# Attention feeding an MLP: the weight-mixing steps are pinned to their place and moved later, attention starts batch 1 at half rate

## The chip, the cores and the metric

The kernel runs on one NeuronCore of one Trainium2 chip. The metric is device time of one execution, in microseconds (us). The core has five engines with one instruction queue each: TensorE (PE; its weight loads are listed apart as PEld), VectorE (DVE), ScalarE (ACT), GpSimd (POOL) and SyncE (SP). In this kernel SP issues nearly all DMAs. An engine takes its queue in order, so an instruction that waits holds up everything behind it.

## The reference

```python
def _attn_ref(q, k, v):                       # 8 batches, 12 heads, 448 tokens, head size 64
    S = q.shape[2]
    scale = 1.0 / np.sqrt(q.shape[-1])
    scores = scale * np.matmul(q, k.transpose(0, 1, 3, 2)) - np.log(S)
    attn = 1.0 / (1.0 + np.exp(-scores))
    return np.matmul(attn, v)

def _moe_ref(x, w_in, w_out):                 # 3584 tokens, 768 -> 2048 -> 768
    h = x @ w_in
    g = np.where(h >= 1, h, np.where(h <= -1, 0.0, (h + 1) ** 2 / 4.0))
    return g @ w_out
```

The attention output of the 12 heads of a batch, laid side by side, is `x` of the MLP. All of it is float32 in and out.

## The kernel before, in words

**Stages.** The batches go one after another. While PE does the MLP of batch b, attention of batch b+1 is woven in, in "pieces": a batch has 6 pairs of heads of 5 pieces, 30 in all (`NPIECE`). A piece is a score product (L393 to L411), a sigmoid (ACT L440 or L443), for later pairs a split of the result into two f16 halves (ACT L451, DVE L452), and the product with v (L484). The MLP of a batch is a list of units. Batch 0 has 48 "up" units (h = x w_in, L708) and 24 "down" units for the first eight of sixteen chunks of w_out (L744; the sums are put aside in DRAM, `part`). Batch 1 has 24 up units, 24 down units that end batch 0 with the other eight chunks, 24 up units and 48 down units, 120 in all. From batch 2 on the up product is done in seven block products instead of eight (L674), which needs mixed sums of w_in.

**Splitting.** Products of f32 accuracy are made of f16 halves. `split` turns a chunk f of a weight into its high half (ACT L270 or L266) and its low half (DVE L271, or POOL L267 and L268 for chunks 1, 7 and 13). The f32 copy of a chunk lies where the halves of the next chunk go, so chunk f+1's ACT step follows chunk f's DVE step: the splits are one long ladder. The first eight chunks of w_out are split under scale `wo0`, the others under `wo1`.

**Mixing.** `mix(i)`, i from 0 to 7, builds the block sums of w_in's chunks i and i+8. DVE adds the halves of both chunks (L618, twice, into tile `mixa`), forms four sums (L622 to L625), ACT and DVE split the result (L631, L632, into `mixs`), SP sends it to DRAM (L635, `blocks`), DVE scales the unmixed parts (four of L641, into `mixp`), and SP sends these (L644). The three tiles share a ring of two buffers (`raww`): the next mix's `mixa` takes the buffer of this one's `mixs` and so waits until its DMA has landed, and its `mixs` takes the buffer of `mixp`. The first three sets of `blocks` are loaded back over w_in at the end of batch 1 (`load_set`, L650), and the scaled x blocks of batch 2 (ACT L533, DVE L534) go over w_in's chunks 10 to 16, so all mixes must have read w_in by then. In the program mix(i) stands at unit `MIX0 + i * (MIX1 - MIX0) // 8` of batch 1: units 8, 17, 27, 36, 46, 56, 65, 75.

**What sets the order.** A planner orders each engine's queue ahead of the run: it goes through the program with priorities in program order and a model of times, and gives an engine with nothing ready an instruction from further down. So an instruction can be placed ahead of its place in the program when its inputs and its buffer are ready. `tc.keep_in_program_order(...)` takes that freedom from an instruction: it stays behind the instructions that precede it in the program on its engine, as done for the weight loads. The order is then fixed for the run, whatever the real times are.

**Pacing of attention.** For each batch `share` gives the part of the batch's attention pieces that are to be done by unit u; it is the running sum of per-unit rates, all 8 in the kernel before, so the 30 pieces are spread evenly over the first `last` units (102 in batch 1).

**Names.** PSUM tiles: `psc` scores (2 buffers), `pav` attention output (1), `mo` with `ph`, `po` and `pm` (3 buffers in one ring). `bend` is the nonlinearity: ACT L721 and L724, DVE L722, L723, L725. `start_blocks` (L516, then `diag` L164) and `finish_blocks` find the scale of x for batch 2: PE L174, DVE L175, `x_s` L134, then L533 and L534.

Of the kernel before, what the change touches and what calls it, by code (L numbers as in the profile page):

```python
# [34 lines left out]
NA = 8  # L35
# [18 lines left out]
SB = 2  # L54
QA = 17
QT = 3
WOP = 6
MIXP = 0
CORN = 10
TP = 1  # L60

DW = 8
MIX0 = 8
MIX1 = 85
Q_PRIO = 72

PM = 9
# [5 lines left out]
def sigmoid_attention_mlp(ctx: ExitStack, tc: tile.TileContext, first_qvk, qkv, w_in, w_out, out_t):  # L73
    nc = tc.nc
# [438 lines left out]
    def start_blocks():  # L513

        xm1 = sml_p.tile([P, 1], F32, tag="xm1", name="xm1", bufs=1)
        nc.vector.tensor_reduce(out=xm1, in_=state["xm"], axis=AX.X, op=ALU.max)  # L516
        return xm1, on_diagonal(xm1)
# [79 lines left out]
    def mix_scales():  # L597

        def keep(tag, in0, s1, op0, s2=None, op1=None):
            n = len(mixed)  # L600
            mixed[tag] = t = mixes[:, n : n + 1]
            nc.vector.tensor_scalar(out=t, in0=in0, scalar1=s1, scalar2=s2, op0=op0, **({"op1": op1} if op1 else {}))
            return t

        low = keep("low", wi.scale[0], wi.scale[1], ALU.min, 0.25, ALU.mult)
        keep("inv", wi.inv[0], wi.inv[1], ALU.max, 4.0, ALU.mult)
        to = [keep("to%d" % k, low, wi.inv[k], ALU.mult) for k in range(2)]
        keep("ratio", wi.scale[1], wi.inv[0], ALU.mult)
        keep("minus", mixed["ratio"], -1.0, ALU.mult)
        mixed["to"] = to  # L610

    def mix(i):

        to, ratio, minus = mixed["to"], mixed["ratio"], mixed["minus"]
        f, g, H = i, i + NFC // 2, DM // 2
        a = raw_p.tile([P, 2 * DM], I32, tag="raww", name="mixa").bitcast(F32).rearrange("p (r n) -> p r n", r=2)
        for r, chunk in ((0, f), (1, g)):
            (nc.gpsimd if r < MIXP else nc.vector).tensor_tensor(  # L618
                out=a[:, r], in0=w_in_sb[:, chunk, 0, :], in1=w_in_sb[:, chunk, 1, :], op=ALU.add
            )  # L620
        a11, a12, a21, a22 = a[:, 0, :H], a[:, 0, H:], a[:, 1, :H], a[:, 1, H:]
        nc.vector.tensor_tensor(out=a22, in0=a21, in1=a22, op=ALU.add)  # L622
        nc.vector.scalar_tensor_tensor(out=a21, in0=a11, scalar=ratio, in1=a21, op0=ALU.mult, op1=ALU.subtract)
        nc.vector.scalar_tensor_tensor(out=a11, in0=a11, scalar=minus, in1=a22, op0=ALU.mult, op1=ALU.add)
        nc.vector.scalar_tensor_tensor(out=a12, in0=a12, scalar=ratio, in1=a11, op0=ALU.mult, op1=ALU.subtract)  # L625
        st = raw_p.tile([P, 2 * DM], I32, tag="raww", name="mixs").bitcast(F16)
        sv = st.rearrange("p (r t h n) -> p r t h n", r=2, t=2, h=2)
        for r in range(2):
            src = a[:, r].rearrange("p (t n) -> p t n", t=2)
            hi = sv[:, r, :, 0, :]  # L630
            nc.scalar.activation(hi, src, AF.Copy, scale=to[1])  # L631
            nc.vector.scalar_tensor_tensor(  # L632
                out=sv[:, r, :, 1, :], in0=src, scalar=to[1], in1=hi, op0=ALU.mult, op1=ALU.subtract
            )
        nc.sync.dma_start(out=blocks[i][:, 3 * DM :], in_=st)  # L635
        pl = raw_p.tile([P, 2 * DM], I32, tag="raww", name="mixp").bitcast(F16)[:, : 3 * DM]
        pv = pl.rearrange("p (t h n) -> p h t n", t=3, h=2)
        for t0, n, chunk, k in ((0, 2, f, 0), (2, 1, g, 1)):
            src = w_in_sb[:, chunk].rearrange("p h (t n) -> p h t n", t=2)[:, :, 2 - n :, :]
            for h in range(2):  # L640
                nc.vector.tensor_scalar(  # L641
                    out=pv[:, h, t0 : t0 + n, :], in0=src[:, h], scalar1=to[k], scalar2=None, op0=ALU.mult
                )
        nc.sync.dma_start(out=blocks[i][:, : 3 * DM], in_=pl)  # L644

    def load_set(n):

        if n < (B - SB) * NFC // 2:
            dst = sets[n % 3].rearrange("p t h n -> p (t h n)")
            nc.sync.dma_start(out=dst, in_=blocks[n % (NFC // 2)])  # L650

    def block_scales(b, inv_x):

        common_scales(b, small("invq", inv_x, 0.25, ALU.mult), small("ihc", inv_x, mixed["inv"], ALU.mult))
# [103 lines left out]
    def ups(b, lo=0, hi=NFC):  # L758
        return [lambda f=f, u=u: up(b, f, u) for f in range(lo, hi) for u in range(NCC // 2)]

    def ups_blocks(b):

        n = NFC // 2
        order = [(0, j) for j in range(4)]
        for i in range(n):
            if i + 1 < n:
                order += [(i + 1, 0), (i + 1, 1)]
            order += [(i, 4), (i, 5), (i, 6)]
            if i + 1 < n:
                order += [(i + 1, 2), (i + 1, 3)]  # L770
        return [lambda i=i, j=j: up_blocks(b, i, j) for i, j in order]

    def downs(b, k=None):
        n = NFC if k is None else GROUPS[k].stop - GROUPS[k].start
        return [lambda m=m, u=u: down(b, m, u, k) for m in range(NCC) for u in range(n // 2)]

    def step(i):

        p, c = divmod(i, NPC)
        late = i >= NPC * (NFULL + NHALF)  # L780
        if c == 0:
            load_pair(p + 3)
            prep_a(p + 2)
        if c == 2:
            prep_b(p + 2)
            if late:
                prep_a(p + 3)
        if i < NPC * (NFULL + NHALF):
            more, some = i + LAG + 1, [i]
        else:  # L790

            more, some = i + 4, [i, i + 1]
            if c % 2:
                return
        more = min(more, B * NPIECE)
        if more > state["scored"]:
            scores(range(state["scored"], more))
            state["scored"] = more
        for k in some:
            av(k)  # L800
# [42 lines left out]
    units = ups(0) + downs(0, 0)  # L843
    x1 = len(units)
    for u, unit in enumerate(units):
# [7 lines left out]
        f, r = divmod(u, NCC // 2)  # L853
# [25 lines left out]
    for b in range(1, B):  # L879
        units = ups_blocks(b) + downs(b)  # L880
        last = len(units) - 96 + LAST
        if b == 1:
            mix_scales()
            units = ups(1, 0, NA) + downs(0, 1) + ups(1, NA, NFC) + downs(1)
            last = len(units) - LAST1
        first = at

        share = [DW if b < SB or u < len(units) - 48 else 8 for u in range(last)]
        share = [sum(share[:u]) / sum(share) for u in range(last + 1)]
        with ExitStack() as order:  # L890
            if b >= PM:
                order.enter_context(tc.manual_schedule(engines={mybir.EngineType.PE}))
            for u, unit in enumerate(units):
                while at < min(b + 2, B) * NPIECE and (at - first) < share[min(u + 1, last)] * NPIECE:
                    step(at)
                    at += 1
                if b == 1:
                    while split_at < min(NFC, NA + (u + 1) * (NFC - NA) // (NA * NCC // 2 - 2)):
                        wo.split(split_at, split_at % WOP == 1)
                        split_at += 1  # L900
                    while mixed_at < NFC // 2 and u >= MIX0 + mixed_at * (MIX1 - MIX0) // (NFC // 2):
                        mix(mixed_at)
                        mixed_at += 1
                if b + 1 < B and u == last:
                    begun = start_blocks()
                unit()
                if b + 1 < B and u == last:
                    inv_x = finish_blocks(*begun)
                    block_scales(b + 1, inv_x)
                if b == 1 and u == last - 2:  # L910
                    for n in range(3):
                        load_set(n)
# [39 lines left out]
```

## Time and profile before

| | |
|---|---|
| median of 3 runs | 1179.65 us (1177.72 to 1180.3) |
| the profiled execution | 1179.06 us, span 1177.3 us |
| PE busy | 1140.0 us, 97% of the span |
| DVE busy | 826.9 us, 70% |
| ACT busy | 699.9 us, 59% |
| POOL busy | 321.1 us, 27% |

The span is what the profile shows from the first to the last instruction; the execution's time is 1.76 us longer. The places that matter here: downs of batch 0 start at 153.05 us on PE, the first up unit of batch 1 at 210.58 us, the downs that end batch 0 at 249.18 us, the first block product of batch 2 at 385.87 us. A row of the timeline gives start, length, engine, line, operation, output and inputs, tile shape, type and count; in brackets the idle time ahead of it and what ended that. A row of the windows view gives for a stretch its length and, for each engine, busy time and number of instructions, then the granted PE clock (1.00 is full), the DMA engines' busy share and GB/s.

### The profile page before, as it was taken

The numbers are of one execution on the slowest core, as the hardware profiler recorded it, in microseconds if no ns is written. First come the engines' busy times: TensorE is split into PE (matmuls) and PEld (weight loads), VectorE is DVE, ScalarE is ACT, GpSimd is POOL, SyncE is SP. The second block draws the span as 40 slices with busy tenths as digits, with TensorE's granted clock in tenths as the row PEclk, the third lists the DMA queues.
The fourth block names the chain that finished last, engine by engine and source line by source line (L and its number), as shares of the span: only waits on it lengthen the run. The fifth ranks groups of instructions, "written<-read, shape, count | busy, mean of one in ns | idle before, by whom it ended". The sixth has DMA issues, their size and how long they took to land.

```text
span 1177.3 us, 20221 instructions
## 1 busy us (share of the span) xinstructions
PE 1140.0 (97%) x7662; PEld 668.5 (57%) x7662; DVE 826.9 (70%) x1758; ACT 699.9 (59%) x1162; POOL 321.1 (27%) x389
## 2 busy tenths in 40 slices
PE   8889988799999999999999999999999999999998
PEld 2234333344445786467854677457764677558954
DVE  6998997997935788368873689367873688736830
ACT  6986984675743686448764577546864486523410
POOL 0025010100341353425353236233533253310000
PEclk9999999999999999999999999999999999999999
DMA  9941643447421465215733166324652256302400
GB/s 358 376 164 62 207 134 138 154 159 245 160 67 55 142 201 204 72 57 166 262 131 92 57 229 200 126 64 143 205 198 67 62 166 213 118 25 101 151 16 32
DMA packets 58113, 170.01 MB, mean 144 GB/s; under 512 B 8608, under 2 KB 39840, under 8 KB 51872
## 3 DMA queue, kind: packets, MB, share of 16 engines
q1 hardware_dynamic: 56288, 159.29, 39.6%
q10 hardware_dynamic: 1728, 9.44, 2.3%
q8 instruction: 60, 0.98, 0.4%
q14 instruction: 37, 0.30, 0.1%
HBM read 126.94 MB, written 23.40 MB: 128 GB/s over the span
## 4 chain that ended last, share of the span: by engine, by line
PE 74%; DVE 6%; DMA 5%; ACT 1%; POOL 1%; issue 1%; SPq 0%; POOLq 0%; ACTq 0%
PE po L744 34%; PE ph L674 23%; PE pav L484 7%; PE psc L402 3%; PE ph L708 3%; PE psc L411 2%; DMA blocks<-mixs 2%; PE psc L397 2%; DMA w_in_sb<-blocks 1%; DVE mixs L632 1%; DMA raw<-qkv 1%; DMA blocks<-mixp 1%; DVE w_out_sb L271 1%; DVE mixa L618 1%; DMA w_out_sb<-w_out 0%
## 5 line engine op out<-in xcount | busy, mean ns | idle before, releaser
L744 PE MATMUL po<-ghl,w_out_sb 128*128 128x448 f16 x2304 | 446.2, 353 | 7.2 <-DVE w_out_sb L271 3.6
L744 PEld LDWEIGHTS <-w_out_sb 128*128 128x128 f16 x2304 | 222.2, 98 | 224.5 <-issue 13.5
L674 PE MATMUL ph<-w_in_sb 128*128 128x224 f16 x3024 | 307.7, 259 | 1.7 <-DMA w_in_sb<-blocks 1.3
L674 PEld LDWEIGHTS <-w_in_sb 128*128 128x128 f16 x3024 | 282.6, 98 | 30.6 <-issue 27.3
L452 DVE SCALAR_TENSOR_TENSOR ahl<-psc,ahl 128x896 f16<-128x896 f32 (+1 forms) x170 | 153.0, 900 | 112.4 <-ACT ahl L451 110.4
L443 ACT ACTIVATE psc<-psc,nls,sqk 128x896 f32<-128x896 f32 (+1 forms) x136 | 129.6, 974 | 114.9 <-PE psc L411 97.1
L364 POOL TENSOR_SCALAR raw<-raw,qkv_s 128x448 f32<-128x448 f32 (+1 forms) x93 | 70.8, 774 | 451.1 <-DVE qkv_i L138 352.1
L451 ACT ACTIVATE ahl<-psc 128x896 f16<-128x896 f32 (+1 forms) x170 | 127.1, 763 | 29.9 <-DVE ahl L452 28.8
L708 PE MATMUL ph<-xhl,w_in_sb 128*128 128x448 f16 x576 | 114.7, 357 | 3.4 <-DVE g L723 2.0
L328 ACT ACTIVATE dump<-raw 128x448 f16<-128x448 f32 (+1 forms) x105 | 62.0, 590 | 77.6 <-DMA raw<-qkv 76.7
L683 DVE TENSOR_TENSOR xhl<-ph,xhl 128x224 f32<-128x224 f32 x240 | 87.8, 383 | 26.0 <-PE ph L674 19.8
L484 PE MATMUL pav<-ahl,v 128*64 128x448 f16 x748 | 96.5, 362 | 0.0
L721 ACT ACTIVATE g<-xhl,hr,ihr 128x448 f32<-128x448 f32 x96 | 69.0, 755 | 43.2 <-DVE xhl L683 42.3
L724 ACT ACTIVATE ghl<-g 128x448 f16<-128x448 f32 x128 | 72.8, 574 | 35.5 <-DVE g L723 35.2
L725 DVE TENSOR_TENSOR ghl<-g,ghl 128x448 f16<-128x448 f32 x128 | 86.8, 686 | 7.9 <-ACT ghl L724 6.6
L708 PEld LDWEIGHTS <-w_in_sb 128*128 128x128 f16 x576 | 55.6, 99 | 64.1 <-issue 16.2
L722 DVE SCALAR_TENSOR_TENSOR g<-g,rk 128x448 f32<-128x448 f32 x112 | 81.8, 745 | 10.6 <-ACT g L721 10.4
L754 DVE TENSOR_SCALAR o<-po,od 128x448 f32<-128x448 f32 x48 | 32.5, 679 | 62.5 <-PE po L744 62.4
L402 PE MATMUL psc<-qk 128*128 128x448 f16 x252 | 66.3, 354 | 7.2 <-ACT a L440 3.6
L366 POOL TENSOR_TENSOR hl<-raw,hl 128x448 f16<-128x448 f32 x62 | 69.6, 1140 | 0.0
L723 DVE SCALAR_TENSOR_TENSOR g<-xhl,ihs,g 128x448 f32<-128x448 f32 x96 | 65.8, 703 | 0.3
L484 PEld LDWEIGHTS <-v 128*64 128x64 f16 x748 | 36.6, 109 | 38.7 <-issue 24.3
(156 smaller groups left out, 1142.5 us busy)
## 6 DMA issues: line engine op xcount, KB each, us to landing
w_in_sb<-blocks SPq DMA_DIRECT2D x48, 1344.0 KB, 6.5
raw<-qkv SPq DMA_DIRECT2D x34, 704.0 KB, 4.8
qk<-hl SPq DMA_DIRECT2D x320, 56.0 KB, 2.0
w_out_sb<-w_in SPq DMA_DIRECT2D x16, 768.0 KB, 11.1
out_t<-o SPq DMA_DIRECT2D x48, 224.0 KB, 1.9
blocks<-mixs SPq DMA_DIRECT2D x8, 768.0 KB, 3.6
w_out_sb<-w_out ACTq DMA_DIRECT2D x6, 768.0 KB, 5.0
raww<-w_out ACTq DMA_DIRECT2D x6, 768.0 KB, 5.0
```

What stands on the lines that cost most here:

```text
L402: nc.tensor.matmul(out, kq[:, j, 1, w], kq[:, j, 0, :], start=True, stop=False)
L443: nc.scalar.activation(a, a, AF.Sigmoid, bias=nls, scale=sqk)
L451: nc.scalar.activation(hi, x, AF.Copy, scale=ATT)
L452: nc.vector.scalar_tensor_tensor(out=lo, in0=x, scalar=ATT, in1=hi, op0=ALU.mult, op1=ALU.subtract)
L484: nc.tensor.matmul(pav[j * D : (j + 1) * D, :S], *terms[j][t], start=c == 0 and t == 0, stop=mid and t == len(terms[j]) - 1,)
L674: nc.tensor.matmul(out, w[:, wt, wh, c * P : (c + 1) * P], xc[:, xt, c, xh, :], start=j in (0, 2) and c + wh + xh == 0, stop=c == HC - 1 a ...
L683: add = lambda out, q, other: nc.vector.tensor_tensor(out=out, in0=quarter(q), in1=other, op=ALU.add)
L708: nc.tensor.matmul(ph[:, :S], w_in_sb[:, f, wh, c * P : (c + 1) * P], xhl[:, c, xh, :], start=c == 0 and wh + xh == 0, stop=c == NCC - 1 a ...
L722: nc.vector.scalar_tensor_tensor(out=g, in0=g, scalar=rt, in1=g, op0=ALU.min, op1=ALU.mult)
L724: nc.scalar.activation(hi, g, AF.Copy)
L725: (nc.gpsimd if f % GPOOL else nc.vector).tensor_tensor(out=ghl[:, f, 1, :], in0=g, in1=hi, op=ALU.subtract)
L744: nc.tensor.matmul(po[:, :S], w_out_sb[:, f, wh, m * P : (m + 1) * P], ghl[:, f, gh, :], start=f == lo and wh + gh == 0, stop=f == hi - 1 ...
```

## The change

The two adds that begin a mix (L618) are made with `keep_in_program_order`, and always on DVE (in the kernel before `MIXP = 0` gave the same). The first mix stands at unit 24 instead of 8 of batch 1, the last at 87 instead of 75: units 24, 33, 42, 51, 60, 69, 78, 87. The attention rate is 4 in the first 24 units of batch 1 and 8 elsewhere. With one constant gone, lines below 58 of the changed kernel have numbers one lower.

```diff
@@ -55,13 +55,12 @@
 WOP = 6
-MIXP = 0
 CORN = 10
 TP = 1
 
 DW = 8
-MIX0 = 8
-MIX1 = 85
+MIX0 = 24
+MIX1 = 96
@@ -615,9 +614,9 @@
         for r, chunk in ((0, f), (1, g)):
-            (nc.gpsimd if r < MIXP else nc.vector).tensor_tensor(
+            tc.keep_in_program_order(nc.vector.tensor_tensor(
                 out=a[:, r], in0=w_in_sb[:, chunk, 0, :], in1=w_in_sb[:, chunk, 1, :], op=ALU.add
-            )
+            ))
@@ -885,7 +884,7 @@
-        share = [DW if b < SB or u < len(units) - 48 else 8 for u in range(last)]
+        share = [DW // 2 if b < SB and u < NA * NCC // 2 else DW for u in range(last)]
         share = [sum(share[:u]) / sum(share) for u in range(last + 1)]
```

How it moves instructions is read from the two orders. First, DVE's queue during the first downs of batch 0 (from about 157 us before). Before, the first mix stands among the splits of w_out (L271):

```order
L239 TENSOR_REDUCE wo_most<-w_out_sb 128x1
L618 TENSOR_TENSOR mixa<-w_in_sb 128x768 x2
L723 SCALAR_TENSOR_TENSOR g<-ph,ihs_570,g 128x448
L271 SCALAR_TENSOR_TENSOR w_out_sb<-w_out_sb,wo_s 128x768
...
L271 SCALAR_TENSOR_TENSOR w_out_sb<-w_out_sb,wo_s 128x768
L618 TENSOR_TENSOR mixa<-w_in_sb 128x768 x2
L251 TENSOR_REDUCE wo_m<-wo_most 128x2
L622 TENSOR_TENSOR mixa<-mixa 128x384
L253 TENSOR_SCALAR wo_x<-wo_m 128x1
L271 SCALAR_TENSOR_TENSOR w_out_sb<-w_out_sb,wo_s 128x768
```

Now the same splits (one line number lower) follow each other:

```order
L270 SCALAR_TENSOR_TENSOR w_out_sb<-w_out_sb,wo_s 128x768 x2
L493 TENSOR_REDUCE xm<-x_92 128x1
L502 TENSOR_REDUCE xm_1700<-xm 128x1
L270 SCALAR_TENSOR_TENSOR w_out_sb<-w_out_sb,wo_s 128x768
L250 TENSOR_REDUCE wo_m<-wo_most 128x2
L252 TENSOR_SCALAR wo_x<-wo_m 128x1
```

Five mixes stood in DVE's queue ahead of the downs that end batch 0; now none does. On PE the part of the queue from the first downs to those downs has 8 score products fewer (two pieces of attention are now behind it).

Second, DVE's queue at the end of batch 1, where x is scaled for batch 2. Before:

```order
L516 TENSOR_REDUCE xm_3296<-xm 128x1
L754 TENSOR_SCALAR o<-po,od 128x448
L164 TENSOR_SCALAR diag<-ident,xm_3296 128x128
L175 TENSOR_REDUCE xm_3296<-psc 128x1
L130 TENSOR_SCALAR x_e<-xm_3296 128x1
```

Now the last mix stands in it:

```order
L515 TENSOR_REDUCE xm_3296<-xm 128x1
L617 TENSOR_TENSOR mixa<-w_in_sb 128x768 x2
L163 TENSOR_SCALAR diag<-ident,xm_3296 128x128
...
L631 SCALAR_TENSOR_TENSOR mixs<-mixa,mixes,mixs 128x2x384
L753 TENSOR_SCALAR o<-po,od 128x448
L631 SCALAR_TENSOR_TENSOR mixs<-mixa,mixes,mixs 128x2x384
L174 TENSOR_REDUCE xm_3296<-psc 128x1
L640 TENSOR_SCALAR mixp<-w_in_sb,mixes 128x2x384 x2
L640 TENSOR_SCALAR mixp<-w_in_sb,mixes 128x384 x2
L129 TENSOR_SCALAR x_e<-xm_3296 128x1
```

The adds of the last mix are ahead of `diag`, and the rest of it is ahead of the scale `x_e`. PE's product of `diag` stands 92 L744 matmuls ahead of the end of batch 1's downs (102 before).

Third, SP's queue around the end of batch 0. Before, the second and third mix's DMAs stand among the stores of batch 0's sums:

```order
L635 DMA blocks<-mixs 128x3072
L756 DMA part<-o 128x448 x2
L644 DMA blocks<-mixp 128x2304
L756 DMA part<-o 128x448 x2
```

Now the first mix's DMAs stand behind the stores and loads of the second half's sums, and later mixes' among the DMAs that lay out q and k for attention:

```order
L755 DMA out_t<-o 128x448
L737 DMA o<-part 128x448
L634 DMA blocks<-mixs 128x3072
L643 DMA blocks<-mixp 128x2304
...
L643 DMA blocks<-mixp 128x2304
L372 DMA qk<-hl 64x448
L634 DMA blocks<-mixs 128x3072
L373 DMA qk<-hl 64x448
L372 DMA qk<-hl 64x448 x2
L643 DMA blocks<-mixp 128x2304
```

Behind the first block product of batch 2 all queues of PE, DVE and ACT hold the same instructions in the same order.

## The prediction

> **What bounds the kernel now.** I read the page's busy shares first, then the chain of waits from 140 us on, then windows over batch 1, and last the timelines around each gap of PE.
>
> ```profile
> span 1177.3 us, 20221 instructions
> PE 1140.0 (97%) x7662; PEld 668.5 (57%) x7662; DVE 826.9 (70%) x1758; ACT 699.9 (59%) x1162; POOL 321.1 (27%) x389
> ...
> 153.00:249.20 96.20, 81.61 (x400) 34.67 (x398) 86.27 (x182) 62.03 (x100) 10.48 (x8) 0.96 0.44 145
> 249.20:385.90 136.70, 134.76 (x752) 65.94 (x751) 90.39 (x190) 71.21 (x119) 30.43 (x39) 0.99 0.41 131
> ```
>
> PE sets the time, with 37 us of idle in the span. Of that, 96.20 - 81.61 = 14.6 us lie in the first stretch (call it A: first downs of batch 0 to the downs that end it), and 1.9 us in the second (B: from there to the first block product of batch 2). In A it is DVE that is full, 86.3 of 96.2 us; in B it has 46 us to spare. Outside A and B the queues are unchanged, so the sum is made of A and B alone. Who holds PE in A:
>
> ```profile
> DVE mixa L618 <- DMA blocks<-mixs: 7.8, 3, 6.1
> PE po L744 <- DVE w_out_sb L271: 3.6, 2, 2.7
> PE ph L708 <- DVE g L723: 2.0, 1, 2.0
> PE pm L158 <- DVE g L723: 1.7, 2, 1.4
> ...
> 180.79 1.83 DVE L618 TENSOR_TENSOR mixa<-w_in_sb 128x768 f32<-128x768 f16 x2 [6.09 <-DMA blocks<-mixs]
> 183.25 1.01 DVE L271 SCALAR_TENSOR_TENSOR w_out_sb<-w_out_sb,wo_s 128x768 f16<-128x768 f32 x1
> 186.49 1.82 POOL L268 TENSOR_TENSOR w_out_sb<-w_out_sb 128x768 f16<-128x768 f32 x1
> 184.31 1.01 PE L744 MATMUL po<-ghl,w_out_sb 128*128 128x448 f16 x3 [2.74 <-DVE w_out_sb L271]
> ```
>
> The second mix's add waits 6.09 us for a DMA, and the split of w_out's seventh chunk (L271) stands behind it in DVE's queue; PE waits for that split, then POOL splits the eighth chunk, ready at 186.49 + 1.82 = 188.3 us. Later PE waits for DVE's L723, which frees a `ph` buffer and stands between the fourth and fifth mix. So mixes that PE does not need before 386 us hold up work that it needs at once.
>
> **What the change removes from A.** No mix is left in A. First by idle time: 14.6 us, of which some stays. The scale of x for batch 1 is a chain of its own:
>
> ```profile
> 204.99 0.22 PE L174 MATMUL pm<-diag,one 128*128 128x128 bf16 x1
> 206.37 0.35 PE L402 MATMUL psc<-qk 128*128 128x448 f16 x1 [0.79 <-DMA qk<-hl]
> 208.21 0.54 PE L402 MATMUL psc<-qk 128*128 128x448 f16 x2 [0.60 <-ACT a L440]
> 210.58 0.73 PE L708 MATMUL ph<-xhl,w_in_sb 128*128 128x448 f16 x3 [0.69 <-ACT xhl L507]
> ```
>
> These gaps (0.79, 0.60, 0.69, and some 0.9 in shorter ones behind) make 3.0 us, and no mix is in their way. 1.1 us are idle from 153 to 158 us (first row of the next view), where the queues are as before, and I leave 1.4 us for the unforeseen. That keeps 5.5, so 9.1 us go. Second the clock:
>
> ```profile
> 153.00:158.00 5.00, 3.87 (x19) 1.23 (x17) 5.00 (x6) 2.91 (x6) 2.95 (x2) 1.00 0.63 182
> 182.00:193.00 11.00, 7.34 (x29) 2.74 (x30) 10.32 (x18) 3.77 (x7) 2.90 (x2) 0.84 0.19 77
> 224.00:229.00 5.00, 1.61 (x10) 0.47 (x7) 5.00 (x10) 3.38 (x6) 2.38 (x1) 1.00 0.01 2
> 229.00:245.00 16.00, 16.00 (x77) 7.74 (x76) 16.00 (x32) 10.97 (x20) 2.24 (x4) 0.89 0.69 235
> ```
>
> Behind a gap of 3.4 us the granted clock is 0.89 for 16 us: 0.11 x 16 = 1.8 us lost; around the gaps of 182 to 193 us it is 0.16 x 11 = 1.8 us. Over A that is 0.04 x 81.6 = 3.3 us, of which I let 2.7 go with the gaps. Third, the 8 score products that leave A took 245.76 - 244.21 = 1.5 us:
>
> ```profile
> 244.21 0.73 PE L402 MATMUL psc<-qk 128*128 128x448 f16 x3
> 245.76 3.58 PE L708 MATMUL ph<-xhl,w_in_sb 128*128 128x448 f16 x18
> ```
>
> Sum for A: 9.1 + 2.7 + 1.5 = 13.3 us less. From the other side, along the ladder of splits: ahead of that L271 DVE does one mix (6.8 us, worked out below) and the add and first sum of the next (1.83 + 0.55), and waits 6.09: 15.3 us. Without them the eighth chunk could be ready at 173 us; laid end to end with what else ACT and DVE have queued there, at their own mean times, I come to some 177 us, 11 us sooner. PE would reach the first up unit of batch 1 some 11 us sooner, and the up units would lose 3.4 us of idle, 1.8 of slow clock and the 1.5 us moved: 17.7 us. I take **14.5 us**, nearer the sum of idle rows.
>
> **What it adds to B.** The 1.5 us of score products come back here. DVE gets the mixes. One costs, from groups between 140 and 386 us that hold all eight:
>
> ```profile
> L632 DVE SCALAR_TENSOR_TENSOR mixs<-mixa,mixes,mixs 128x768 f16<-128x768 f32 x16 | 17.4, 1099 | 0.4 <-ACT mixs L631 0.4
> L618 DVE TENSOR_TENSOR mixa<-w_in_sb 128x768 f32<-128x768 f16 x16 | 14.7, 958 | 9.7 <-DMA blocks<-mixs 9.7
> L641 DVE TENSOR_SCALAR mixp<-w_in_sb,mixes 128x768 f16<-128x768 f16 x16 | 5.9, 413 | 0.1
> L625 DVE SCALAR_TENSOR_TENSOR mixa<-mixa,mixes 128x384 f32<-128x384 f32 x8 | 5.5, 682 | 0.1
> L624 DVE SCALAR_TENSOR_TENSOR mixa<-mixa,mixes 128x384 f32<-128x384 f32 x8 | 4.9, 616 | 0.1
> L623 DVE SCALAR_TENSOR_TENSOR mixa<-mixa,mixes 128x384 f32<-128x384 f32 x8 | 4.9, 613 | 0.0
> L622 DVE TENSOR_TENSOR mixa<-mixa 128x384 f32<-128x384 f32 x8 | 4.4, 552 | 0.0
> L641 DVE TENSOR_SCALAR mixp<-w_in_sb,mixes 128x384 f16<-128x384 f16 x16 | 4.4, 312 | 0.0
> ```
>
> That is 62.1 / 8 = 7.8 us, less where instructions overlap at their ends, about 6.8 us. Three mixes are in B now, so five come in: 34 to 39 us on top of 90.4, 124 to 129 of 138 us. DVE's room is nearly gone, and worse than it looks, since its queue is in order and the last stretch of B is fixed:
>
> ```profile
> 358.89 0.24 DVE L164 TENSOR_SCALAR diag<-ident,xm 128x128 bf16<-128x128 bf16 x1
> 363.82 0.22 PE L174 MATMUL psc<-diag,one 128*128 128x128 bf16 x1
> 363.87 19.46 PE L744 MATMUL po<-ghl,w_out_sb 128*128 128x448 f16 x102
> 371.44 0.92 DVE L534 SCALAR_TENSOR_TENSOR w_in_sb<-x,x_s,w_in_sb 128x672 f16<-128x672 f32 x1
> 385.87 6.21 PE L674 MATMUL ph<-w_in_sb 128*128 128x224 f16 x63
> 365.00:385.90 20.90, 20.90 (x118) 10.60 (x117) 10.73 (x36) 6.59 (x9) 0.00 (x0) 1.00 0.09 34
> ```
>
> Before, `diag` is made 4.9 us ahead of PE's product, and x's blocks are ready 13.5 us ahead of the first block product. Now PE's product stands about 118 us into B, and DVE has 124 to 129 less 10.7 for the tail, that is 113 to 118 us of work ahead of `diag`, and its waits on top. What waits: the next mix's add waits until `mixs` has landed.
>
> ```profile
> DMA to landing us min/median/max: 3.2/3.6/8.5
> ```
>
> By summing the rows of the new order, DVE has 3 to 9 us of other work between the last split of one mix and the add of the next. With landings of 3.6 us it waits next to nothing, with 8.5 us about 3.5 us at each of seven places, 24.5 us in all. Before, the waits are 9.7 us for eight mixes, 1.2 each, so I take 8.5 us. DVE then reaches `diag` 121 to 127 us into B against 118, at the low end by the overlap and because the bends at B's start fall into PE's lead: 3 to 6 us late, and PE stops there (L174 cannot be passed), with L744 and all of the following attention queued behind it. Earlier lateness is taken up by three PSUM buffers, a down sum of 24 products being 24 x 19.46 / 102 = 4.6 us. I take **4.5 us**; the ends are -1.9 us (B's idle gone) and +20.5 us (landings of 8.5 us everywhere). x's blocks keep cover: 92 products and a piece of attention, 20 us, lie behind L174, while scale and first block need 8 us. SP's queue holds attention's DMAs behind a mix's until DVE has finished it; they are for a pair that PE reaches a pair (some 25 us) later, so I cost this at nothing, and the lateness of the mix if the cover is gone.
>
> A row speaks against the move: one L632 took more than twice its usual time, beside POOL's L268 above.
>
> ```profile
> L632 DVE SCALAR_TENSOR_TENSOR mixs<-mixa,mixes,mixs x16: 1005/1012/2389, 169.2 to 301.0; 128x768 f16<-128x768 f32 x16
> 345.00:365.00 20.00, 20.00 (x113) 10.01 (x112) 7.33 (x20) 6.42 (x12) 10.44 (x13) 1.00 0.27 83
> ```
>
> [...]
>
> **The sum.** On the profiled execution's 1179.06 us (0.6 us under the median of the three): -14.5 + 1.5 + 4.5 = -8.5, so **1170.6 us**.
>
> **The rivals.** (1) *B takes the mixes for nothing.* DVE's spare time in B speaks for it; the time is 1179.06 - 14.5 + 1.5 = 1166 us, 1163 with the 17.7. (2) *DVE becomes the bound of B: slower.* At the ring of two buffers each add waits for a landing of 8.5 us, as where a load of raw q, k, v ran beside it, and POOL's bursts lengthen DVE's work. `diag` is 20.5 us late: 1179.06 - 14.5 + 1.5 + 20.5 = 1186.6 us. It turns to a loss when `diag` is over 13 us late, from about 2.4 us of wait a mix. Against it: four of the eight adds waited not at all. (3) *A was not held by the mixes.* The ladder of splits and x's scale hold PE anyway; only the waits that name DVE's L271 and L723 go, 7.3 us with 1.5 moved: -8.8 + 6.0 in B = 1176 to 1178 us. Against it: the 6.09 us wait sits in the ladder itself. (4) *The pin does nothing, the planner placing mixes early still*: the order rules it out.
>
> **How the numbers follow.** The forecast (1167 to 1174.5) gets 0.50, rival 1 0.27, rival 2 0.14, rival 3 0.09. Range: 1161.5 (ladder's 17.7 and B's idle gone) to 1181 (part of rival 2). A run of this kernel can be told from no change beyond 0.2%, 2.4 us. Faster: 0.50 + 0.27 and a little of rival 3, 0.78; same 0.08; slower 0.14.
>
> **What would show it.** Right: no L618 ahead of the up units' end; PE idle ahead of them under 7 us; the downs that end batch 0 start at 233 to 237 us instead of 249.2; DVE busy over 120 us in B; PE idle 5 to 8 us in B, the longest gap at L174 waiting for `diag`. Wrong: the first downs' PE gaps stay (rival 3), B's PE idle under 2.5 us (rival 1) or over 14 us with L618 waiting for `mixs` each time (rival 2).

## The result, and the profile after

The changed kernel takes **1169.67 us** (median of 4 runs, 1167.77 to 1170.52) where the kernel before takes 1179.75 us (4 runs, 1177.72 to 1180.3): ratio **0.9915**, 95% interval 0.9898 to 0.9933. The profiled execution took 1170.52 us; the forecast against the profiled execution of before was 1170.6 us. First the page's span and shares, then the windows of A and B:

```profile
span 1168.8 us, 20224 instructions
PE 1139.1 (97%) x7662; PEld 668.3 (57%) x7662; DVE 833.9 (71%) x1758; ACT 699.1 (60%) x1162; POOL 324.6 (28%) x389
...
152.45:234.75 82.30, 79.01 (x390) 34.10 (x389) 54.98 (x126) 50.70 (x82) 9.80 (x8) 0.96 0.29 86
234.75:376.97 142.22, 136.57 (x759) 66.28 (x758) 130.17 (x246) 82.52 (x135) 35.16 (x39) 1.00 0.50 175
```

A begins 0.6 us earlier and is 13.8 us shorter (96.13 us before, 153.05 to 249.18 us). B is 5.5 us longer (136.69 us before). What follows B is 0.4 us longer: -0.6 - 13.8 + 5.5 + 0.4 = -8.5 us of span. PE's idle time goes from 14.6 to 82.30 - 79.01 = 3.3 us in A and from 1.9 to 142.22 - 136.57 = 5.65 us in B. DVE has the mirror image: 86.2 us of work in A before, 55.0 now, and in B 90.4 before, 130.2 now.

The gaps of PE over 0.5 us, by the timeline, A in the first three rows and B in the last four:

```profile
158.09 3.15 PE L743 MATMUL po<-ghl,w_out_sb 128*128 128x448 f16 x8 [1.13 <-DVE g L722]
200.08 0.54 PE L401 MATMUL psc<-qk 128*128 128x448 f16 x2 [0.70 <-ACT a L439]
202.45 12.00 PE L707 MATMUL ph<-xhl,w_in_sb 128*128 128x448 f16 x54 [0.70 <-ACT xhl L506]
...
305.38 0.73 PE L396 MATMUL psc<-hl,w_in_sb 128*128 128x448 f16 x3 [2.23 <-DVE ahl L451]
307.70 8.11 PE L743 MATMUL po<-ghl,w_out_sb 128*128 128x448 f16 x42 [0.72 <-DVE g L722]
339.93 0.54 PE L401 MATMUL psc<-qk 128*128 128x448 f16 x2 [0.99 <-issue]
356.80 0.23 PE L173 MATMUL psc<-diag,one 128*128 128x128 bf16 x1 [1.33 <-DVE diag L163]
```

In A PE no longer waits for DVE's splits of w_out (0.2 us for one of ACT's is the most), and the up units (202 to 235 us) run without a gap. In B the longest gap is not at `diag` but at L396, which waits for DVE's L451. The chain of waits from 290 to 310 us says what L451 stood behind:

```profile
298.58 1.04 DVE mixp L640 x2
299.62 0.74 issue
300.36 2.21 DVE mixp L640 x2
302.57 0.63 DVE ghl L724
303.20 0.53 DVE xm L493
303.73 0.59 DVE g L721
304.32 1.00 DVE ahl L451
```

The four scalings of a mix (L640) are the longest link, 1.04 + 2.21 us. The timeline shows one such group 20 us earlier, this one, and what POOL did meanwhile:

```profile
279.09 1.20 DVE L640 TENSOR_SCALAR mixp<-w_in_sb,mixes 128x768 f16<-128x768 f16 x4
298.50 4.07 DVE L640 TENSOR_SCALAR mixp<-w_in_sb,mixes 128x768 f16<-128x768 f16 x4
298.51 0.61 POOL L364 TENSOR_SCALAR v<-raw 128x512 f16<-128x512 f32 x1
299.09 2.24 POOL L365 TENSOR_TENSOR hl<-raw,hl 128x448 f16<-128x448 f32 x2
301.29 1.17 POOL L365 TENSOR_TENSOR v<-raw,v 128x512 f16<-128x512 f32 x1
```

1.20 us became 4.07 us, and the group ended as POOL ended the split of an attention pair. The groups at 319.55 and 347.95 us, beside the next two splits, took 2.53 and 2.62 us. By the groups of DVE from 140 to 377 us:

```profile
L617 DVE TENSOR_TENSOR mixa<-w_in_sb 128x768 f32<-128x768 f16 x16 | 16.2, 1052 | 1.4 <-DMA blocks<-mixs 1.4
L640 DVE TENSOR_SCALAR mixp<-w_in_sb,mixes 128x768 f16<-128x768 f16 x16 | 8.0, 543 | 0.1
L640 DVE TENSOR_SCALAR mixp<-w_in_sb,mixes 128x384 f16<-128x384 f16 x16 | 7.9, 533 | 0.0
L622 DVE SCALAR_TENSOR_TENSOR mixa<-mixa,mixes 128x384 f32<-128x384 f32 x8 | 6.1, 768 | 0.2
```

The eight groups of the mixing add up to 69.3 us against 62.1 us before: +7.2 us for the same instructions. The waits for a landing of `mixs`, 9.7 us before, are 1.4 us.

### The profile page after: what moved, and what is told of

Its sections match the earlier page's. It is cut to its first block, busy times and chain, and to the rows that moved or that the text cites. A ratio compares the mean times of both kernels' runs of the same rounds, so it can differ in the third digit from the quotient of the medians.

```text
span 1168.8 us, 20224 instructions
## 1 busy us (share of the span) xinstructions
PE 1139.1 (97%) x7662; PEld 668.3 (57%) x7662; DVE 833.9 (71%) x1758; ACT 699.1 (60%) x1162; POOL 324.6 (28%) x389
## 4 chain that ended last, share of the span: by engine, by line
PE 69%; DVE 8%; DMA 5%; ACT 3%; POOL 2%; issue 1%; SPq 0%; POOLq 0%; ACTq 0%; DVEq 0%
PE po L743 31%; PE ph L673 23%; PE pav L483 7%; PE psc L401 3%; PE ph L707 2%; PE psc L410 2%; DMA raw<-qkv 2%; PE psc L396 1%; DVE ahl L451 1%; DMA w_in_sb<-blocks 1%; DVE mixa L617 1%; DVE mixp L640 1%; ACT psc L442 1%; POOL hl L365 1%; ACT dump L327 1%
## 5 line engine op out<-in xcount | busy, mean ns | idle before, releaser
L743 PE MATMUL po<-ghl,w_out_sb 128*128 128x448 f16 x2304 | 447.9, 353 | 3.0 <-DVE g L722 1.9
L743 PEld LDWEIGHTS <-w_out_sb 128*128 128x128 f16 x2304 | 222.3, 98 | 220.5 <-issue 18.0
L451 DVE SCALAR_TENSOR_TENSOR ahl<-psc,ahl 128x896 f16<-128x896 f32 (+1 forms) x170 | 152.9, 899 | 98.9 <-ACT ahl L450 96.9
L450 ACT ACTIVATE ahl<-psc 128x896 f16<-128x896 f32 (+1 forms) x170 | 126.9, 762 | 30.9 <-DVE ahl L451 29.8
L723 ACT ACTIVATE ghl<-g 128x448 f16<-128x448 f32 x128 | 72.6, 573 | 42.9 <-DVE g L722 42.5
L483 PE MATMUL pav<-ahl,v 128*64 128x448 f16 x748 | 96.4, 360 | 0.0
L707 PEld LDWEIGHTS <-w_in_sb 128*128 128x128 f16 x576 | 55.4, 98 | 59.9 <-issue 11.3
L722 DVE SCALAR_TENSOR_TENSOR g<-xhl,ihs,g 128x448 f32<-128x448 f32 x96 | 66.0, 704 | 0.3
L483 PEld LDWEIGHTS <-v 128*64 128x64 f16 x748 | 36.4, 109 | 37.7 <-issue 23.2
```

The costliest lines, as they stand in the source:

```text
L450: nc.scalar.activation(hi, x, AF.Copy, scale=ATT)
L451: nc.vector.scalar_tensor_tensor(out=lo, in0=x, scalar=ATT, in1=hi, op0=ALU.mult, op1=ALU.subtract)
L483: nc.tensor.matmul(pav[j * D : (j + 1) * D, :S], *terms[j][t], start=c == 0 and t == 0, stop=mid and t == len(terms[j]) - 1,)
L707: nc.tensor.matmul(ph[:, :S], w_in_sb[:, f, wh, c * P : (c + 1) * P], xhl[:, c, xh, :], start=c == 0 and wh + xh == 0, stop=c == NCC - 1 a ...
L743: nc.tensor.matmul(po[:, :S], w_out_sb[:, f, wh, m * P : (m + 1) * P], ghl[:, f, gh, :], start=f == lo and wh + gh == 0, stop=f == hi - 1 ...
```

## The experiments

| kernel | A begins | A | B | PE idle in A, B | ratio to before (95%) |
|---|---|---|---|---|---|
| before | 153.05 | 96.1 | 136.7 | 14.6, 1.9 | 1 |
| changed | 152.45 | 82.3 | 142.2 | 3.3, 5.65 | 0.9915 (0.9898 to 0.9933) |
| changed, again | 152.09 | 81.9 | 142.05 | 4.3, 4.4 | 0.9922 (0.9910 to 0.9935) |
| tie alone | 152.63 | 85.9 | 138.5 | 7.7, 3.6 | 0.9941 (0.9923 to 0.9959) |
| later alone | 150.96 | 95.7 | 136.6 | 14.0, 1.75 | 1.0005 (0.9993 to 1.0016) |
| half rate alone | 152.87 | 96.5 | 137.6 | 15.1, 1.6 | 1.0012 (0.9999 to 1.0025) |
| tie and later | 152.12 | 82.0 | 144.6 | 3.8, 7.8 | 0.9964 (0.9947 to 0.9981) |
| before without mixing arithmetic | 159.46 | 81.0 | 133.4 | 4.2, 0.0 | 0.9906 (0.9884 to 0.9928) |
| the same, transfers tied | 151.91 | 82.5 | 133.4 | 4.2, 0.0 | 0.9868 (0.9848 to 0.9888) |
| changed, scalings on ACT | 151.96 | 81.2 | 142.5 | 5.0, 3.9 | 0.9941 (0.9924 to 0.9958) |
| changed, mixes to unit 88 | 154.33 | 82.6 | 142.7 | 4.8, 3.3 | 0.9952 (0.9936 to 0.9969) |
| changed, three splits off POOL | 152.68 | 82.35 | 140.45 | 4.5, 2.4 | 0.9923 (0.9906 to 0.9941) |
| changed, three splits off POOL, scalings on ACT | 152.18 | 83.2 | 137.6 | 4.0, 0.0 | 0.9889 (0.9871 to 0.9907) |
| changed, three splits off POOL, first mix at 16 | 154.60 | 80.1 | 140.2 | 3.1, 3.4 | 0.9938 (0.9925 to 0.9950) |

A and B are read from one profile each, in us; idle is length less PE busy.

### Which part of the change does it

**The tie alone.**

```diff
-            (nc.gpsimd if r < MIXP else nc.vector).tensor_tensor(
+            tc.keep_in_program_order(nc.vector.tensor_tensor(
```

> The kernel before with only the two sums at the head of each step of the mixing tied to their place in the program; the steps stay spread over units 8 to 85 of batch 1 and attention keeps its rate. In the order of VectorE's instructions six steps started before the downs that end batch 0; here two do. Theory (the steps of the mixing on VectorE are what holds stretch A, the units from the first downs of batch 0 to the downs that end it): most of A's gain comes already from this, A goes from 96.1 us to 84 to 88 us, stretch B from 136.7 to 139 to 142 us, the whole to 1168 to 1174 us. Rival (attention's rate brings the gain, since its score products stand in front of the down products): A stays within 3 us of 96.1 and the time within 1177 to 1181 us.

1169.92 us against 1176.54 us before. Windows of A and B:

```profile
152.63:238.54 85.91, 78.23 (x394) 33.69 (x393) 66.94 (x147) 57.92 (x95) 11.07 (x8) 0.98 0.32 100
238.54:377.06 138.52, 134.88 (x756) 65.80 (x754) 116.71 (x227) 76.83 (x125) 35.33 (x39) 1.00 0.50 170
```

A and the time are as the theory had it, and B is half a microsecond under its range. In time two mixes start in A here (at 198.0 and 231.6 us), five before. The first block product of batch 2 starts at 377.06 us, in the changed kernel at 376.97 us. By the ratios the tie gives 0.59% and the whole change 0.78 to 0.85%, with intervals that overlap: the tie by itself carries most of the gain, and what the rest adds to it can't be told from noise.

**Later alone.**

```diff
-MIX0 = 8
-MIX1 = 85
+MIX0 = 24
+MIX1 = 96
```

> The kernel before with only the two numbers changed that place the steps of the mixing (units 24 to 96 of batch 1 in place of 8 to 85), not tied. The order of the instructions on SyncE and GpSimd is the same as in the kernel before, and on VectorE the steps of the mixing start behind the same neighbours as before. Theory: without the tie the later place in the program moves nothing, A stays at 96.1 us within 1 us and the time is the same, 1177 to 1181 us. Rival (the place in the program alone acts): 1169 to 1174 us.

1176.51 us against 1176.54 us: no difference. Where an instruction may be moved forward in its queue, its place in the program decided nothing here.

**Half rate alone.**

```diff
-        share = [DW if b < SB or u < len(units) - 48 else 8 for u in range(last)]
+        share = [DW // 2 if b < SB and u < NA * NCC // 2 else DW for u in range(last)]
```

> The kernel before with only attention's rate halved in the first 24 units of batch 1; the mixing is untouched, and six of its steps still start in stretch A. Theory: A keeps its idle time of 14.6 us and loses only the eight score products that move out of it, 1 to 3 us; B gains the same; the time is 1176 to 1181 us, not to be told from before. Rival (the rate brings the gain): A 84 to 88 us, the time 1168 to 1173 us.

1178.32 us against 1176.54 us; the theory's range holds it. A did not get shorter even by the eight score products: PE's busy time stays (81.53 us before, 81.42 us here, at a granted clock of 0.96 and 0.95) and its idle time is 15.1 us.

**Tie and later, attention's rate as before** (the two diffs above together).

> The changed kernel with attention's rate as it was before (the steps of the mixing tied and later, nothing else). Theory: A is as short as in the changed kernel but for the score products that stay in it, 83 to 86 us against 82.3; B is shorter by them, 139 to 142 us against 142.2; the time is 1167 to 1172 us, as the changed kernel's 1169.7. Rival (the rate carries the gain, the mixing only makes room for it): 1175 to 1180 us.

1171.95 us against 1176.54 us, at the upper edge of the theory's range. A is even shorter than expected (82.0 us against 83 to 86), B was missed:

```profile
234.11:378.75 144.64, 136.82 (x755) 66.21 (x753) 128.21 (x244) 78.64 (x127) 35.09 (x39) 0.99 0.50 172
...
346.40 3.29 DVE L641 TENSOR_SCALAR mixp<-w_in_sb,mixes 128x768 f16<-128x768 f16 x4
353.98 2.87 DVE L618 TENSOR_TENSOR mixa<-w_in_sb 128x768 f32<-128x768 f16 x2
357.07 0.29 PE L174 MATMUL psc<-diag,one 128*128 128x128 bf16 x1 [3.63 <-DVE diag L164]
```

Here the wait at `diag` is 3.63 us, behind a group of scalings of 3.29 us and two adds of 2.87 us (1.82 us elsewhere). Against the tie alone, the later place takes 3.9 us more out of A and puts 6.1 us more into B. The half rate brings 2.4 us of that back in B. By the ratios (0.9964 here, 0.9915 and 0.9922 with the half rate, intervals apart) it brings some 5 us, more than this one profile of the fastest of six executions shows. So it is worth something only together with the later place; why it shortens B is not settled by these runs.

### How much the mixing can cost at all

**Before, without the mixing's arithmetic.**

```diff
-        a = raw_p.tile([P, 2 * DM], I32, tag="raww", name="mixa").bitcast(F32).rearrange("p (r n) -> p r n", r=2)
...
-        nc.sync.dma_start(out=blocks[i][:, : 3 * DM], in_=pl)
+        for s, chunk in enumerate((i, i + NFC // 2)):
+            src = w_in_sb[:, chunk].rearrange("p h n -> p (h n)")
+            nc.sync.dma_start(out=blocks[i][:, 3 * DM + 2 * DM * s : 3 * DM + 2 * DM * (s + 1)], in_=src)
...
```

> The kernel before with the arithmetic of the mixing left out: VectorE's and ScalarE's part of each step is gone, and the two transfers per step take as many bytes straight from w_in's tiles, so the blocks of batches 2 and later hold unmixed weights (that part of the result is left out). The steps stay where they were. It gives the most that any placing of the steps can bring. Theory (VectorE's time in the mixing is what A and B lose): A 80 to 84 us against 82.3 in the changed kernel, B 135 to 137 us against 142.2 there and 136.7 before, the whole some 5 us under the changed kernel, 1161 to 1167 us on a chip where before takes 1177. Rival (A is held by the splitting of w_out and of the inputs on ScalarE, not by the mixing): A stays above 90 us, the time above 1172 us.

1166.63 us against 1177.03 us. A and B came out as expected (81.0 and 133.4 us), the sum did not: the transfers, which no longer waited for arithmetic, went out among the loads of the input, the first one at 49.74 us, and A began at 159.46 us. So the same kernel with those transfers tied:

```diff
-            nc.sync.dma_start(out=blocks[i][:, 3 * DM + ...], in_=src)
+            tc.keep_in_program_order(nc.sync.dma_start(out=blocks[i][:, 3 * DM + ...], in_=src))
```

> The kernel before with VectorE's and ScalarE's arithmetic of the mixing left out again (the blocks of batches 2 and later hold unmixed weights, so that part of the result is left out), and now the transfers in its place tied to theirs: in the run without the tie they went out from 50 us on and A began 6.4 us later. Theory (that delay alone kept the run without arithmetic at 1166.6 us): A begins at 152 to 154 us, A takes 80 to 82 us and B 132 to 135 us as there, the time is 1158 to 1163 us on a chip where before takes 1177. Rival (the transfers themselves cost the time, wherever they go out): 1164 to 1169 us.

1162.89 us against 1179.37 us, in the theory's range; A is 0.5 us above it:

```profile
151.91:234.41 82.50, 78.30 (x394) 33.87 (x393) 56.66 (x129) 54.44 (x91) 9.53 (x8) 0.98 0.37 112
234.41:367.84 133.43, 133.43 (x755) 66.06 (x753) 68.19 (x148) 66.13 (x111) 28.21 (x39) 1.00 0.50 171
```

That is the ceiling: 1.32% for the mixing's whole arithmetic. Of this the changed kernel gets 0.78 to 0.85 percentage points. Its A is as short as here, and its B is 8.8 us longer (what follows B is 1.6 us shorter), so what is left lies in B. B has no PE idle here.

### What B pays for

**The four scalings on ACT.**

```diff
-                nc.vector.tensor_scalar(
-                    out=pv[:, h, t0 : t0 + n, :], in0=src[:, h], scalar1=to[k], scalar2=None, op0=ALU.mult
-                )
+                nc.scalar.activation(pv[:, h, t0 : t0 + n, :], src[:, h], AF.Copy, scale=to[k])
```

> The changed kernel with the four scalings of each step of the mixing that write the plain blocks (1.20 us for four on VectorE alone, 2.5 to 4.1 us where GpSimd splits an attention pair at the same time) moved to ScalarE. Theory (B's loss of 5.5 us is VectorE drawn out beside GpSimd: the two longest waits of TensorE in B, 2.23 us and 0.72 us, stand right behind the 4.07 us of such a group): these waits go, B falls from 142.2 by 2 to 4 us and the time is 1165 to 1168 us where the changed kernel takes 1169.7. Rival (VectorE's sheer amount of work in B, 130 of 142 us): VectorE loses about 16 us of work, and B falls by as much or more. Second rival (ScalarE becomes late instead, since every split, sigmoid and gate waits for it): 1169 to 1175 us.

1169.80 us against 1177.03 us, and B is 142.5 us: neither the theory's fall of 2 to 4 us nor the rival's larger one; the time lies in the second rival's range. DVE lost 10 us of work in B (120.0 us). The timeline beside POOL's split, and two of PE's gaps:

```profile
301.62 3.34 POOL L365 TENSOR_TENSOR hl<-raw,hl 128x448 f16<-128x448 f32 x2
302.28 3.50 DVE L617 TENSOR_TENSOR mixa<-w_in_sb 128x768 f32<-128x768 f16 x2
304.93 1.87 POOL L365 TENSOR_TENSOR v<-raw,v 128x512 f16<-128x512 f32 x1
305.70 1.08 DVE L451 SCALAR_TENSOR_TENSOR ahl<-psc,ahl 128x896 f16<-128x896 f32 x1
...
306.83 0.73 PE L396 MATMUL psc<-hl,w_in_sb 128*128 128x448 f16 x3 [0.25 <-POOL v L365]
356.28 0.23 PE L173 MATMUL psc<-diag,one 128*128 128x128 bf16 x1 [2.18 <-DVE diag L163]
```

With L640 gone, the next mix's adds stand beside POOL, and their two instructions take 3.50 us instead of 1.82. The remaining mixing instructions on DVE take 57.2 us; with the splits off POOL too (below) the same take 50.3 us. What POOL's splits add is again 7 us, on other instructions. The two waits that the theory named did go (0.25 us is left at L396 and 0.1 us at the downs), and yet B kept its length: the wait at `diag` grew from 1.33 to 2.18 us, 0.84 us came at L483 for ACT's L450, and PE's busy time is 138.6 us where the changed kernel's two profiles have 136.6 and 137.7. Closing the longest gap did not give its time back.

**Three pairs' splits off POOL.**

```diff
-QA = 17
+QA = 20
```

> The changed kernel with the splits of the next three attention pairs that GpSimd does (its work from about 294, 319 and 345 us) given to ScalarE and VectorE instead; VectorE has three instructions of about 0.7 us more per pair, some 6 us in all. Theory (VectorE is drawn out beside GpSimd): the scalings of the mixing take 1.20 us for four everywhere, VectorE's work in B changes by less than 3 us in all, and the time is the changed kernel's within 2.5 us, 1167 to 1172 us. Rival (only the amount of VectorE's work counts, GpSimd draws nothing out): VectorE's work in B grows by 6 us, from 130 to 136 of 142, the scalings still take 2.5 us and more in places, and B grows by 3 to 6 us, the time to 1172 to 1176 us.

1168.57 us against 1177.03 us, inside the theory's range. The groups of four take 1.20 us, but for one that stands beside POOL's other work, on x:

```profile
297.89 1.20 DVE L640 TENSOR_SCALAR mixp<-w_in_sb,mixes 128x768 f16<-128x768 f16 x4
349.51 2.55 DVE L640 TENSOR_SCALAR mixp<-w_in_sb,mixes 128x768 f16<-128x768 f16 x4
349.67 1.72 POOL L529 TENSOR_TENSOR xhl<-x,xhl 128x672 f32<-128x672 f32 x1 [0.79 <-DVE xhl L528]
...
306.57 1.27 PE L396 MATMUL psc<-hl,w_in_sb 128*128 128x448 f16 x3 [2.36 <-DVE ahl L451]
```

Nine instructions of 0.7 us came to DVE, and yet its work in B fell from 130.2 to 127.9 us. But PE still waits 2.36 us at L396, now without a drawn-out group ahead. In its place DVE's queue holds the three splits that came over from POOL (L359, 2.1 us from 297.3 us on). So the drawing out was real, but this run puts as much other work in the same spot, and doesn't say how much of the wait it made.

**Both together** (the two diffs above).

> The changed kernel with both: the splits of three attention pairs given to ScalarE and VectorE, and the mixing's plain scalings given to ScalarE. Theory (what is left of B's loss is VectorE's: its work, and the part drawn out beside GpSimd): VectorE's work in B falls from 128 to about 118 us, the waits of TensorE in B from 5.65 us to under 2.5 us, the time to 1163 to 1167 us where before takes 1177. Rival (ScalarE is late now, with 2.8 us more per step and 2 us more per pair, above 105 of 140 us in B): waits of TensorE for ScalarE in B of 3 us and more, 1168 to 1173 us.

```profile
235.38:373.02 137.64, 137.64 (x760) 65.61 (x758) 116.53 (x223) 108.30 (x176) 11.29 (x12) 1.00 0.51 175
```

No PE idle is left in B, and DVE's work there is 116.5 us, as the theory had it. Three of four executions took 1163.44, 1166.18 and 1167.93 us; one took 3141.43 us, for which no trace shows a reason, and the ratio leaves it out. On the same chip before took 1179.37 us and the changed kernel 1169.72 us (1167.74 to 1172.15). The ratio 0.9889 (0.9871 to 0.9907) lies just clear of the changed kernel's 0.9922 (0.9910 to 0.9935). It is faster than the kernel before; that it is also some 0.3% faster than the changed one is likely but rests on three executions, the slowest of which reaches into the changed kernel's range. Neither edit was run on the kernel before, so what they would give without the moved mixes is open. The rival (ScalarE late) falls: ACT has 108.3 of 137.6 us, and PE waits for it nowhere in B. B is still 4.2 us above the ceiling's 133.43 us; by the groups of PE, four score products more are in it (2.0 us), and the rest lies inside busy time (the 100 products L483 with v take 14.2 us here and 11.2 us there), unexplained.

**The changed kernel again.**

> The changed kernel once more, beside the others on one chip. Its ratio to before was 0.9915 with an interval of 0.9898 to 0.9933; the same is expected, 0.990 to 0.993, and in the trace A 81 to 84 us, B 140 to 144 us, and four scalings of the mixing drawn out to 2.5 us or more for the steps that stand beside GpSimd's splits of attention pairs.

It repeats: 1169.72 us, A 81.88 us, B 142.05 us, the same three drawn-out groups.

**Other places for the mixes.** The last one earlier:

```diff
-MIX1 = 96
+MIX1 = 88
```

> The changed kernel with the steps of the mixing spread over units 24 to 88 instead of 24 to 96 of batch 1. In the order of VectorE's instructions the last four steps each start a few instructions earlier; the last one is then started ahead of the second last's neighbours and not right before the product that puts the scales of x together. Theory: the wait of TensorE for that scale (1.33 us in the changed kernel) goes, the waits beside GpSimd stay; the time is 1167 to 1170 us. Rival (the steps crowd VectorE more when they stand closer): B grows by 1 to 4 us, 1170 to 1174 us.

1171.06 us against 1177.03 us; the profiled execution was the slowest of six (1173.96 us). The wait at `diag` went and the waits at 308 to 311 us stayed (2.68 and 0.66 us), as the theory said, but the time is in the rival's range. B grew by only 0.5 us, though, and A began 1.9 us later than in the changed kernel, which nothing in the edit explains; between the two this run doesn't decide. And the first one earlier, with the three splits off POOL (`QA = 20`):

```diff
-MIX0 = 24
+MIX0 = 16
```

> The changed kernel with the splits of three attention pairs given to ScalarE and VectorE, and the first step of the mixing at unit 16 of batch 1 in place of 24, the others between it and unit 96 as before: one step now starts in the last third of A, where VectorE has room, and the steps in B stand further apart. Theory (the steps are taken for nothing wherever VectorE has room, in A after the batch's input is split): A stays within 1.5 us of 82.3 us, B falls by 1 to 3 us below the 140.45 us of the run with those splits alone, the time is 1164 to 1168 us where before takes 1177. Rival (any step in A holds the up units again): A grows by 2.5 us or more, and the time is 1169 us or more.

1171.10 us against 1179.37 us. With a mix in it A is no longer than without (80.1 us), so the rival falls; B gained 0.3 us only, with waits of 1.29 us for ACT's L450 and 1.50 us for DVE's L722, and the time is above the theory's range. Here too A began late, at 154.60 us.

## Why the prediction was right, and where not

**A: -14.5 us forecast, -13.8 measured.** The mechanism is shown three ways: the tie alone shortens A, the two other parts alone don't, and without arithmetic A has the same 81 to 82.5 us. Rival 3 (A not held by the mixes) falls. Inside the term the sizes were off. Idle lost 11.3 us, not 9.1: 3.3 us stayed of the 5.5 that I kept. Busy time lost 2.5 us, where 1.5 us of score products and 2.7 us of clock were forecast; the clock gave nothing in this profile (0.96 of full before and after), and in the second profile it is 0.98. That the sum of the term fits so closely is luck: the two errors point opposite ways. The other count, along the ladder, was too long: the eighth chunk is ready at 179.8 us, 8.5 us sooner and not 11, and the first up unit starts 8.1 us sooner; the up units themselves gained 6.3 us where 6.7 were counted. One reading in it is off as well: the L723 that PE waits for at 229 us stands inside the fourth mix, ahead of its scalings, and not behind it.

**B: +6.0 us forecast, +5.5 measured.** +1.8 us are busy time. The eight score products are seen in the groups of PE in B, first after, then before:

```profile
L401 PE MATMUL psc<-qk 128*128 128x448 f16 x30 | 8.1, 352 | 1.4 <-issue 1.0 <-DVE qkv_e L129 0.4
L410 PE MATMUL psc<-hl 64*128 64x448 f16 x30 | 5.4, 359 | 0.0
```

```profile
L402 PE MATMUL psc<-qk 128*128 128x448 f16 x26 | 6.7, 357 | 1.9 <-DVE qkv_e L130 1.9
L411 PE MATMUL psc<-hl 64*128 64x448 f16 x26 | 4.4, 372 | 0.0
```

Four more of each. The other 3.7 us are idle, forecast 4.5. The size was right by luck, the step under it wrong: I built it of 8.5 us of waits for `mixs` to land, and put the loss at `diag`. Measured were 1.4 us of such waits. In their place DVE's mixing instructions were drawn out by 7.2 us beside POOL, and PE lost 2.95 us at L396 and L743 (how much of the wait at L396 comes from that stays open, as said at the run with three splits off POOL) and 1.33 us at `diag`. DVE's load was a little over what I counted (130.2 us; 124 to 129 forecast). The lower end of the range comes to 1161.0 us by its own terms, not 1161.5.

**What would show it.** No L617 ahead of the up units' end: the first is at 239.01 us, yes. PE idle ahead of them under 7 us: 3.3. The downs that end batch 0 at 233 to 237 us: 234.75. PE idle of 5 to 8 us in B: 5.65, but 4.4 in the second profile. Longest gap at `diag`: no, in either profile.

**The row that spoke against it.** One L632 took 2389 ns beside POOL's L268, where the median is 1012 ns; the sum has no term for it. The runs show more of the kind: the longest single L617 is 1.78 us in the changed kernel and 0.96 us with the splits off POOL, while L451, which reads the PSUM tile `psc`, stays under 1.1 us in both from 285 to 365 us. Why the one is drawn out and the other is not, no run shows. Over the eight mixes it comes to 7.2 us of DVE's time. Of PE's time it cost less, since DVE had some room left (130.2 us of work in B's 142.2): 4.4 us of B are what the run with both edits saves on the same chip's 142.05 us, and part of that is DVE's smaller load. Not separated: the splits off POOL alone, and the scalings on ACT alone, can't be told from the changed kernel.

**The rivals.** Rival 1 (B for nothing, 1166 us) did not come about in the changed kernel; with both edits B is 0.95 us longer than before, where rival 1 put 1.5. Rival 2 (B as the bound, slower) was far off: landings of `mixs` held the changed kernel's ring for 1.4 us in all.

## What to carry to other kernels

Work that nobody needs soon, given to an engine by a planner that fills gaps, can hold up work that is needed at once; a tie to its place in the program moved it, and a later place without the tie moved nothing. Where such work is moved to, look at what the neighbouring engine does there: the same instructions took 7 us more beside it. A remaining cost may need two edits at once: taking some of the drawn-out instructions away, or their neighbour, changed nothing that could be told; both together left PE no idle time in that stretch.

## What was not expected of the hardware

In the stretches measured here the clock is lost in helpings of about 3.4 us at 0.50, or not at all behind the same gap. Windows of 1 us behind the 1.13 us gap at 157 to 159 us, first in the changed kernel, then in the one with the scalings on ACT (clock third from the end):

```profile
157.00:158.00 1.00, 0.00 (x0) 0.00 (x0) 1.00 (x3) 1.00 (x2) 0.00 (x0) 0.98 0.94 258
158.00:159.00 1.00, 0.91 (x3) 0.41 (x3) 1.00 (x4) 1.00 (x2) 0.00 (x0) 0.50 0.95 375
...
160.00:161.00 1.00, 1.00 (x4) 0.37 (x3) 0.80 (x3) 1.00 (x3) 0.00 (x0) 0.50 0.00 0
161.00:162.00 1.00, 1.00 (x7) 0.28 (x5) 0.96 (x1) 1.00 (x4) 0.00 (x0) 0.81 0.00 0
```

```profile
158.00:159.00 1.00, 0.02 (x1) 0.00 (x0) 1.00 (x2) 1.00 (x2) 0.00 (x0) 1.00 0.96 172
159.00:160.00 1.00, 0.85 (x5) 0.48 (x5) 1.00 (x3) 1.00 (x2) 0.00 (x0) 1.00 1.04 424
```

The granted clock is 0.50 for about 3.4 us (157.97 to 161.37 us) and then full again, a loss of 1.7 us; behind the same gap in the other kernel it stays at 1.00. The changed kernel's first profile has a second such stretch from 202.3 to 205.6 us, its second profile none there. So two profiles of one kernel differ by such a helping in A. The kernel before has two in A (184.6 to 188.0 and 229.0 to 232.4 us), as many as the changed kernel's first profile, which is why the clock term gave nothing; three other runs have none there (clock 1.00). The forecast's clock term of 2.7 us should have been counted in helpings of 1.7 us, with a chance for each. The drop at 157.97 us comes at the end of the 1.13 us gap, with PE busy for 1.91 of the 3.40 us ahead of it. Why the clock dropped there and not behind the same gap in the other kernel, no run shows.
